# One fused kernel (long convolution and gated dense block) with its instructions in another order

## The chip, the cores and the metric

The kernel runs on one core of a Trainium2 chip. The core has five engines that run side by side, each through its own queue in the order in which the program issues to it: TensorE (PE, matmuls and transposes, which write to PSUM), VectorE (DVE), ScalarE (ACT), GpSimd (POOL) and SyncE (SP, which here only issues DMAs). They wait for each other through semaphores. The metric is the time of one execution on the device, in microseconds (us).

## The reference, cut to what matters

```python
def _A_ref(q, k, v, shift_k, ssm_k, ssm_D):          # S = 2048, D = 640
    k_pad = jnp.pad(k, ((0, 0), (ks - 1, 0), (0, 0)))            # ks = 4
    for t in range(ks):
        k_shift = k_shift + k_pad[:, t:t + S, :] * shift_k[:, ks - 1 - t][None, None, :]
    kv = k_shift * v
    # y = causal convolution of kv with ssm_k along S, by FFTs of length 2 S
    y = y + kv * ssm_D[None, None, :]
    return q * y
def _B_ref(x, w1, b1, w2):                           # F = 1728
    h = jnp.einsum("bsd,df->bsf", x, w1) + b1
    sp = jnp.log1p(jnp.exp(-jnp.abs(h))) + jnp.where(h > 0, h, jnp.zeros_like(h))
    return jnp.einsum("bsf,fd->bsd", h * jnp.tanh(sp), w2)
h = x + _A_ref(_layernorm(x, axis=-1), A_k, A_v, A_shift_k, A_ssm_k, A_ssm_D)    # x = A_q
h2 = h + _B_ref(_layernorm(h, axis=-1), B_w1, B_b1, B_w2)
return h2
```

## The kernel before

The program first builds a list of named steps (`OP(name, engines, dependencies, psum, ...)`), each of which issues one or a few instructions. Then `_ordered` reads the text `ORDER` and emits the steps one after the other in exactly that order, which fixes the order of every engine's queue and of the DMA queue. A token is a step's name. `@n` says which of four PSUM slots of 1024 float32 columns a PE step writes to; `:a`, `:d` or `:p` puts a step on ACT, DVE or POOL where the first of its listed engines isn't meant. A step that reuses a slot waits until the step that copies the old contents out of it is done. The names, in the order of the computation (dc, m and b count five groups of 128 channels, t counts 16 tiles of 128 positions):

- `d_n`, `d_k`, `d_v`, `d_g`, `d_x`, `d_t2m`, `d_a12`, `d_w1`, `d_w2`: loads (L319) of ssm_k, k, v, the table of the second Fourier stage in eight parts, x, two more tables and the weights.
- `dadd`, `k1pe`, `k1ev`: ssm_D is added to the first tap, ssm_k is transposed on PE (L370) and copied out.
- `s1kpe`, `s1kev`, `s2kpe`, `s2kev`: the two Fourier stages of the filter on PE (L390, L391 and L416), each with a copy out of PSUM by ACT (L256) or DVE (L258). Every step of s2k needs all twenty copies of s1k.
- `ktpe`, `ktev`, `ktsh`, `kspe`, `kv`: k is transposed (L335) and copied, one shifted copy is made on POOL, the short convolution runs as matmuls (L351, L352) with weights that `coef` and `wsh0` to `wsh3` (L311) build, and `kv` multiplies with v (L356).
- `s1vpe`, `s1vev`, `s2v0`, `s2v1`, `s2v2`: the same two stages for kv, the second in three chunks of channels (groups 0 and 1, group 2, groups 3 and 4).
- `sw`: two DMAs per group (L444) swap even and odd partitions of the filter's transform; they wait for all of s2k. `pr`: the product of both transforms, four steps per group on DVE (L455).
- `i1pe`, `i1ev`, `i2pe` (`i2a`, `i2b`), `y`: the two inverse stages (L473, L525) and their copies.
- `ln1`, `ln1p`, `lnx`: statistics and layer norm of x; `wb`, `h`, `bn`, `pow`, `hc`: product with it, residual, and second layer norm of a tile; `tr` (by DMA, L557) or `trpe` and `trev` (tiles 0 and 1): its transpose.
- `m1pe`, `hb`, `m2pe`, `res`, `d_out`: first dense layer (L582, L589) in five units of 256, 256, 512, 512 and 512 positions, Mish on ACT (L604), second dense layer (L647, L655), residual (L669, L672) and store.

Of the kernel before, what the change touches and what calls it, by code (L numbers as in the profile page):

```python
# [25 lines left out]
ORDER = """
d_dr wz idn d_n0 cz wm@0 small lane d_n1 d_cst d_sk d_n2 warm d_n3 d_n4 kz dsel d_g3 dcol dadd0 d_k0 k1pe0@1 d_k3 dadd1 k1pe1@2 d_k1 k1ev0 d_k2 k1ev0b
s1kpe0_0@3 k1ev1 s1kpe0_3@0 s1kev0_0 dadd2:p d_v3 s1kpe0_1@1 s1kev0_3 s1kev0_1:d s1kpe0_2@2 dadd3:p d_g6 s1kpe1_0@3 s1kev0_2 k1pe2@0 dadd4:p d_g7
s1kev1_0 cfpe@1 k1pe3@2 coef k1ev2:a s1kpe1_3@3 k1ev3 wsh0 k1pe4@1 d_v0 s1kev1_3 s1kpe2_0@0 k1ev4 s1kpe2_1@2 d_v2 s1kev2_0 wsh2 s1kpe3_0@3 s1kpe4_3@1
s1kev2_1 s1kev3_0:d s1kpe4_0@0 d_v1 s1kev4_3 s1kpe2_2@2 s1kev4_0:d wsh1 s1kpe3_1@3 s1kev2_2 ktpe2_0@1 d_g1 ktpe2_3 s1kev3_1:d ktpe4_0@0 ktpe4_1  # L30
ktpe1_0@2 ktpe4_3 ktpe1_1 wsh3 d_g0 ktpe4_2 ktpe1_2 ktev4 ktpe1_3 ktpe2_2 ktpe2_1 ktpe3_0@3 ktev2:a ktpe3_1 d_g4 ktev1 ktsh4 ktpe3_3 ktpe3_2
s1kpe3_2@0 ktev3 ktsh1 s1kpe4_1@2 d_g2 s1kev3_2 ktpe0_0@1 ktpe0_1 ktsh3 ktpe0_2 s1kev4_1 s1kpe1_2@3 d_g5 ktsh2 s1kpe1_1@0 s1kev1_2:d ktpe0_3 s1kev1_1
kspe3_1@2 ktev0 s1kpe4_2@3 s1kpe2_3@0 s1kev4_2 kv3_1 ktsh0 s1kpe3_3@1 s1kev2_3:d kspe4_0@3 s1kev3_3 kspe3_0@2 kv4_0 s2kpe_126@0 s2kpe_102@1
s2kev_126:d s2kpe_18@3 s2kev_102 kv3_0 kspe2_0@0 s2kev_18 s2kpe_0@1 kv2_0 s2kpe_48@2 s2kev_0 kspe0_0@3 s2kev_48 s2kpe_24@0 kv0_0 kspe1_0@1 s2kev_24
s2kpe_96@2 kv1_0 s2kpe_54@3 s2kev_96 kspe2_1@0 s2kev_54:d d_x0 s2kpe_36@1 d_x1 s2kpe_6@2 s2kev_36 kv2_1 kspe1_1@3 s2kev_6 s2kpe_66@1 kv1_1 s2kpe_84@0
s2kev_66 kspe4_1@2 s2kev_84 s2kpe_120@3 kv4_1 s2kpe_42@1 s2kev_120 kspe0_1@0 ln1_2 s2kev_42 s2kpe_72@2 s1vpe2_3@3 s2kev_72 kv0_1 ln1p2 s2kpe_60@1
s1vev2_3 s2kpe_30@2 s2kev_60:d d_x3 s1vpe0_1@0 s2kev_30 s1vpe2_0@3 s1vev0_1:d s1vpe1_2@1 s1vev2_0 s1vpe0_0@2 s1vev1_2:d s1vpe1_3@0 s1vev0_0
s2kpe_114@3 s1vev1_3 ln1_0 s1vpe3_0@2 s2kpe_12@1 s2kev_114 s1vev3_0:d s2kpe_108@0 s2kev_12 s2kpe_78@3 s2kev_108:d s2kpe_90@2 s2kev_78 s1vpe2_2@1
s2kev_90:d s1vpe0_2@0 s1vev2_2 lnx2:p s1vpe4_1@3 ln1p0 s1vev0_2 sw0_0 s1vpe1_1@2 s1vev4_1:d s1vpe0_3@1 sw1_1 s1vev1_1 s1vpe1_0@0 ln1_1 d_a12
s1vpe3_2@3 sw0_1 s1vev0_3 s1vpe2_1@2 sw3_1 s1vev1_0:d lnx0:p s1vev3_2 sw1_0 s1vpe4_2@1 ln1_3 sw4_1 ln1p1 s1vpe3_3@0 s1vev2_1 s2v0pe_80@3 sw3_0  # L40
s1vev4_2 s1vev3_3:d sw2_1 s2v0pe_64@2 ln1p3 sw2_0 s2v0ev_64 s2v0pe_96@1 s2v0ev_80:d s2v0pe_48@0 lnx3:p s2v0ev_96 s2v0pe_16@2 pr0_64 lnx1:p s1vpe4_3@3
s2v0ev_48 s1vpe3_1@1 s1vev4_3:d s2v0ev_16 s1vpe4_0@0 s1vev3_1 pr1_64 s2v0pe_0@2 s2v0pe_112@3 s1vev4_0 s2v0pe_32@1 s2v0ev_0:d s2v0ev_112 s2v2pe_0@0
pr0_0 s2v2pe_32@2 s2v2ev_0 pr0_96 s2v0ev_32 s2v2pe_96@3 s2v2ev_32 pr1_32 s2v1pe_96@0 s2v2ev_96 s2v1pe_32@1 pr1_0 s2v1ev_96 s2v2pe_16@2 pr1_96
s2v1pe_64@3 s2v1ev_32 s2v1pe_0@0 s2v2ev_16 pr0_32 i1pe1_3@1 s2v1ev_64 pr2_96 s2v1ev_0 s2v2pe_64@2 s2v2pe_112@3 i1ev1_3:d s2v2ev_64 s2v2pe_48@0 pr2_0
s2v2pe_80@1 s2v2ev_48 i1pe0_1@2 d_w11 s2v2ev_112 pr3_0 sw4_0 i1pe0_3@0 d_w10 i1ev0_1 pr2_32 i1pe1_2@3 d_x2 s2v2ev_80 d_w13 i1pe1_0@2 d_t2m pr2_64
i1ev0_3 d_w12 i1pe0_2@1 d_w14 pr3_96 i1ev1_0 i1pe1_1@0 i1ev1_2 pr3_32 i1pe0_0@2 i1ev1_1 pr3_64 i1pe2_0@3 i1ev0_0 i1pe2_3@0 pr4_64 i1ev0_2 i1pe3_0@2
pr4_96 i1ev2_3 i1pe3_2@1 i1ev3_0 pr4_32 i1pe2_2@0 i1ev3_2 pr4_0 i1pe3_1@2 i1ev2_0 i1pe2_1@1 ln1_8 i1ev2_2 i1pe3_3@3 ln1_5 i1ev3_1 ln1p8 i1pe4_3@0
i1ev2_1 ln1_7 i1pe4_2@2 ln1p5 i1ev4_3 ln1_6 i1pe4_1@1 lnx5:p i1ev3_3 i1pe4_0@0 i1ev4_2:d ln1p7 i1ev4_1 i2a0@3 d_w2b ln1_11 b1pe@2 i1ev4_0 i2a1@1 d_w2c
ln1p6 d_w2a ln1_12 c_b1 i2b0 i2b1 i2pe10@0 y0 i2a2@2 y1 wb0 i2b2 i2pe7@3 h0 y10 wb1 i2pe15@1 y2 h1 i2pe9@0 y7 bn1 i2a3@2 y9 i2pe14@3 y15 bn0 i2b3 pow1
i2pe6@0 y3 i2pe5@1 y6 wb2 i2pe11@2 pow0 hc1 y5 wb3 trpe1@0 y11 i2pe8@1 hc0 h3 trev1:a trpe0@2 bn3 trev0:a i2pe4@0 y14 m1pe0_4@2 h2 pow3 y8 bn2 lnx7  # L50
ln1p12 m1pe0_6@3 m1pe0_3@1 hc3 hb0_6 ln1_4 hb0_4 tr3 pow2 m1pe0_0@3 hb0_3 lnx6:p hc2 wb7 lnx8 tr2 m1pe0_1@2 ln1p11 ln1_10 hb0_0 m1pe0_2@1 hb0_1 h7
ln1p10 ln1_15 m1pe0_5@3 hb0_2 ln1p4 bn7 lnx12 m1pe1_3@2 hb0_5 wb5 ln1p15 m1pe1_0@1 ln1_13 hb1_3 lnx11 m1pe1_5@3 wb6 ln1p13 h6 y4 m1pe1_4@2 bn6 hb1_5
lnx15:p lnx4 m1pe1_2@0 h5 pow7 ln1_9 hb1_4 pow6 m1pe1_1@3 hb1_0 wb4 w2z hb1_2 m1pe1_6@2 hc7 bn5 tr7 lnx10:p hb1_1 i2pe12@1 hb1_6 h4 i2pe13@0 wb8 y12
m2pe1@3 h8 bn4 lnx13 y13 wb11 pow4 hc6 h11 pow5 hc4 ln1_14 ln1p9 tr4 m2pe3@2 bn11 ln1p14 tr6 lnx9 hc5 pow11 bn8 lnx14 tr5 wb12 pow8 wb14 m2pe0@1 res3
wb10 d_out3 wb15 hc11 hc8 tr11 h10 h12 m1pe2_5@0 wb9 bn10 bn12 pow10 m1pe2_4@2 hb2_5 h9 pow12 hc10 wb13 tr10 h13 m1pe2_0@0 bn9 hb2_4 tr8 h14 pow9 bn13
m1pe2_3@2 hb2_0 hc9 pow13 hc12 tr9 bn14 m2pe2@0 hb2_3 tr12 hc13 pow14 res1 hc14 d_out1 h15 tr13 bn15 pow15 m1pe2_6@2 res2 res0 d_out2 hc15 d_out0
m1pe2_1@3 hb2_6 tr14 tr15 m1pe3_6@0 m1pe3_4@1 hb3_6 m1pe2_2@2 hb3_4 hb2_1 m1pe3_1@0 hb2_2 m1pe3_2@1 hb3_1 m1pe3_3@3 m1pe3_5@2 hb3_3 m1pe3_0@0 hb3_5
hb3_2 m2pe4@3 hb3_0 m2pe6@2 m2pe5@1 res6 res4 d_out4 d_out6 m2pe7@0 m1pe4_6@2 res5 res7 d_out5 d_out7 m1pe4_5@3 hb4_6 m1pe4_3@1 m1pe4_1@0 hb4_3 hb4_5
m1pe4_4@2 hb4_1 m1pe4_2@1 hb4_4 m1pe4_0@3 hb4_2 m2pe9@0 hb4_0 m2pe11@2 m2pe15a@1 res9 res11 d_out11 d_out9 m2pe8@3 res15a d_out15a m2pe10@0 m2pe12@2
res8 res10 d_out8 d_out10 m2pe14@1 m2pe13@3 res12 res14 d_out12 d_out14 m2pe15b@0 res13 d_out13 res15b d_out15b  # L60
""".split()
# [656 lines left out]
```

## Time and profile before

| what | value |
|---|---|
| median of 3 runs | 227.34 us (227.21 to 227.75) |
| the profiled execution | 227.22 us |
| its span | 225.2 us |
| granted TensorE clock | 1.00 in every stretch |
| busy: PE, DVE, ACT, POOL | 214.5, 137.9, 131.8, 51.4 us |
| loaded from and written to HBM | 20.42 and 2.62 MB |

The span is counted from the first to the last instruction of the profile; about 2 us lie around it. Times in the profile are from the start of the span. A row of a timeline has the start, the duration, the engine, the line and the operation, with output and inputs and their shapes, a count for rows that were merged, and in brackets how long the engine stood idle before it and for whom. In the chain of work that ended last, a row is the start, the duration and what ran; the chain goes back from the last instruction to what released it. Ends of matmuls are modelled.

### The profile page before, as it was taken

The numbers are of one execution on the slowest core, as the hardware profiler recorded it, in microseconds if no ns is written. First come the engines' busy times: TensorE is split into PE (matmuls) and PEld (weight loads), VectorE is DVE, ScalarE is ACT, GpSimd is POOL, SyncE is SP. The second block draws the span as 40 slices with busy tenths as digits, with TensorE's granted clock in tenths as the row PEclk, the third lists the DMA queues.
The fourth block names the chain that finished last, engine by engine and source line by source line (L and its number), as shares of the span: only waits on it lengthen the run. The fifth ranks groups of instructions, "written<-read, shape, count | busy, mean of one in ns | idle before, by whom it ended". The sixth has DMA issues, their size and how long they took to land.

```text
span 225.2 us, 6200 instructions
## 1 busy us (share of the span) xinstructions
PE 214.5 (95%) x2684; PEld 157.5 (70%) x2690; DVE 137.9 (61%) x250; ACT 131.8 (59%) x180; POOL 51.4 (23%) x102
## 2 busy tenths in 40 slices
...
DMA packets 19563, 30.98 MB, mean 138 GB/s; under 512 B 10704, under 2 KB 14928, under 8 KB 18768
## 3 DMA queue, kind: packets, MB, share of 16 engines
...
q10 hardware_dynamic: 336, 0.12, 0.3%
...
HBM read 20.42 MB, written 2.62 MB: 102 GB/s over the span
## 4 chain that ended last, share of the span: by engine, by line
PE 69%; DVE 9%; ACT 8%; issue 6%; DMA 5%; POOL 1%; SPq 1%; DVEq 0%; ACTq 0%
PE ps L647 26%; PE ps L582 25%; ACT uv L256 5%; PE ps L473 4%; PE ps L390 3%; ACT ks L256 3%; DVE ra L356 3%; DVE ks L455 3%; DMA ks<-ks 3%; PE ps L335 2%; DMA ks<-in_A_ssm_k_dram 2%; PE ps L370 2%; DVE uv L258 2%; PE ps L589 1%; PE ps L655 1%
## 5 line engine op out<-in xcount | busy, mean ns | idle before, releaser
L604 ACT ACTIVATE ks<-ps,b1s 128x512 bf16<-128x512 f32 (+1 forms) x69 | 35.9, 605 | 43.2 <-PE ps L589 22.9
L647 PE MATMUL ps<-ks 128*128 128x320 bf16 (+2 forms) x420 | 58.6, 299 | 0.0
L582 PE MATMUL ps<-G 128*128 128x512 bf16 (+1 forms) x319 | 57.2, 336 | 0.4
L672 DVE TENSOR_TENSOR rb<-ps,rb 128x640 bf16<-128x640 f32 x15 | 11.8, 819 | 68.3 <-PE ps L655 65.9
L647 PEld LDWEIGHTS <-ks 128*128 128x128 bf16 x420 | 40.6, 98 | 17.4 <-issue 1.3
L582 PEld LDWEIGHTS <-G 128*128 128x128 bf16 x325 | 31.4, 98 | 24.5 <-issue 1.4
L256 ACT CAST uv<-ps 128x1024 bf16<-128x1024 f32 x49 | 45.5, 1089 | 0.5 <-ACT uv L256 0.4
L256 ACT CAST ks<-ps 128x960 bf16<-128x960 f32 (+2 forms) x47 | 39.0, 910 | 8.6 <-PE ps L391 6.1
L455 DVE TENSOR_TENSOR ks<-ks,uv 128x2048 bf16<-128x2048 bf16 x20 | 23.1, 1218 | 1.2 <-DMA ks<-ks 1.2
L416 PEld LDWEIGHTS <-G 128*128 128x128 bf16 x512 | 20.5, 96 | 4.5 <-issue 3.8
L473 PE MATMUL ps<-a_t,ks 128*128 128x128 bf16 x320 | 18.2, 219 | 0.8 <-DVE ks L455 0.8
L473 PEld LDWEIGHTS <-ks 128*128 128x128 bf16 x320 | 18.0, 113 | 0.9 <-DVE ks L455 0.9
L542 POOL TENSOR_TENSOR r<-ve,mhalf 128x1 f32<-128x1 f32 x16 | 10.5, 661 | 22.7 <-DVE ve L540 22.7
L416 PE MATMUL ps<-uv,G 128*128 128x64 bf16 (+1 forms) x384 | 12.4, 187 | 2.5 <-DVE uv L258 1.9
L538 DVE BATCH_NORM_STATS2 st<-rb 128x6 f32<-128x320 bf16 x32 | 14.0, 479 | 0.2
L509 POOL TENSOR_SCALAR ve<-mv 128x1 f32<-128x1 f32 x16 | 4.2, 260 | 43.2 <-DVE mv L505 42.1
L504 DVE BATCH_NORM_STATS2 st<-rb 128x6 f32<-128x320 bf16 x32 | 13.8, 473 | 0.0
L258 DVE CAST uv<-ps 128x1024 bf16<-128x1024 f32 x11 | 13.0, 1202 | 0.2 <-ACT uv L256 0.2
L258 DVE CAST ks<-ps 128x1024 bf16<-128x1024 f32 (+2 forms) x11 | 12.1, 1126 | 1.6 <-PE ps L391 1.6
L356 DVE TENSOR_TENSOR ra<-ps,rb 128x1024 bf16<-128x1024 f32 x10 | 12.0, 1219 | 1.2 <-PE ps L352 0.9
L416 PE MATMUL ps<-ks,G 128*128 128x160 bf16 x128 | 11.2, 230 | 0.6 <-DVE ra L356 0.2
L390 PE MATMUL ps<-cst,ra 128*64 128x128 bf16 x160 | 11.0, 219 | 0.5 <-ACT uv L256 0.4
...
## 6 DMA issues: line engine op xcount, KB each, us to landing
ks<-ks SPq DMA_DIRECT2D x10, 512.0 KB, 6.0
G<-tab_g SPq DMA_DIRECT2D x8, 512.0 KB, 11.3
ks<-in_A_ssm_k_dram SPq DMA_DIRECT2D x5, 512.0 KB, 6.1
...
```

Source lines behind the costliest of these rows:

```text
L256: nc.scalar.copy(o, i)
L258: nc.vector.tensor_copy(o, i)
L356: nc.vector.tensor_tensor(kv_w[:, m, :, 8 * h:8 * h + 8, :], p_.f32().rearrange("p (l t d) -> p d t l", l=4, t=8), raw_v[:, 8 * h:8 * h + ...
L390: nc.tensor.matmul(ps[0:64, dgl, :], lhs, mc, start=True, stop=True)
L416: nc.tensor.matmul(p_.f32()[:, o:o + n], g_v[:, f, :], src[:, :, f, :], start=True, stop=True)
L455: nc.vector.tensor_tensor(o, o, v, ALU.mult)
L473: nc.tensor.matmul(pz[:, dgl, :], KS[:, k, b, :, l], a12[:, k, :], start=k == 0, stop=k == 1)
L504: nc.vector.bn_stats(st1[:, t, hh, :], xt(t)[:, hh * 320:(hh + 1) * 320])
L538: nc.vector.bn_stats(st2[:, t, hh, :], xt(t)[:, hh * 320:(hh + 1) * 320])
L582: nc.tensor.matmul(ph[:, o:o + w], w1[:, dc, fc * P:fc * P + P], lt[:, dc, 0:w], start=dc == 0, stop=dc == NDC - 1)
L604: nc.scalar.activation(hb[:, fc, 0:n], p_.f32()[:, i * 512:i * 512 + n], ACT.Mish, bias=b1s[:, fc:fc + 1], scale=1.0)
L647: nc.tensor.matmul(p_.f32()[:, o:o + n], lhs, w2[:, k, cols:cols + n], start=fc == 0, stop=single and fc == 13)
```

## The change

`ORDER` is replaced. The steps are the same, each issues the same instructions, and each engine gets as many steps as before (214 on PE, 166 on DVE, 145 on ACT, 56 on POOL, 76 DMAs of SP). Different are the order in which they are issued, the PSUM slot of most PE steps, and the engine of some: the copies that DVE makes are others than before (16 go from DVE to ACT and 14 from ACT to DVE, i1 and before), `wsh2` moves from POOL to DVE, `dadd1` from DVE to POOL, `dadd2` and `dadd3` from POOL to DVE, `lnx10` from POOL to ACT and `lnx4`, `lnx11` and `lnx14` from ACT to POOL. The loads go out in the order n0 n1 n3 n2 n4 g2 k1 k0 k2 k3 v0 g4 g0 v1 v3 v2 g1 a12 g5 g6 g3 g7 where it was n0 to n4 g3 k0 k3 k1 k2 v3 g6 g7 v0 v2 v1 g1 g0 g4 g2 g5. The last part, from `m2pe14` on, has the same order. Cut to the part up to m1 in the new text (the old text: up to the first steps of s2k):

```diff
 ORDER = """
-d_dr wz idn d_n0 cz wm@0 small lane d_n1 d_cst d_sk d_n2 warm d_n3 d_n4 kz dsel d_g3 dcol dadd0 d_k0 k1pe0@1 d_k3 dadd1 k1pe1@2 d_k1 k1ev0 d_k2 k1ev0b
-s1kpe0_0@3 k1ev1 s1kpe0_3@0 s1kev0_0 dadd2:p d_v3 s1kpe0_1@1 s1kev0_3 s1kev0_1:d s1kpe0_2@2 dadd3:p d_g6 s1kpe1_0@3 s1kev0_2 k1pe2@0 dadd4:p d_g7
-s1kev1_0 cfpe@1 k1pe3@2 coef k1ev2:a s1kpe1_3@3 k1ev3 wsh0 k1pe4@1 d_v0 s1kev1_3 s1kpe2_0@0 k1ev4 s1kpe2_1@2 d_v2 s1kev2_0 wsh2 s1kpe3_0@3 s1kpe4_3@1
-s1kev2_1 s1kev3_0:d s1kpe4_0@0 d_v1 s1kev4_3 s1kpe2_2@2 s1kev4_0:d wsh1 s1kpe3_1@3 s1kev2_2 ktpe2_0@1 d_g1 ktpe2_3 s1kev3_1:d ktpe4_0@0 ktpe4_1
-ktpe1_0@2 ktpe4_3 ktpe1_1 wsh3 d_g0 ktpe4_2 ktpe1_2 ktev4 ktpe1_3 ktpe2_2 ktpe2_1 ktpe3_0@3 ktev2:a ktpe3_1 d_g4 ktev1 ktsh4 ktpe3_3 ktpe3_2
-s1kpe3_2@0 ktev3 ktsh1 s1kpe4_1@2 d_g2 s1kev3_2 ktpe0_0@1 ktpe0_1 ktsh3 ktpe0_2 s1kev4_1 s1kpe1_2@3 d_g5 ktsh2 s1kpe1_1@0 s1kev1_2:d ktpe0_3 s1kev1_1
-kspe3_1@2 ktev0 s1kpe4_2@3 s1kpe2_3@0 s1kev4_2 kv3_1 ktsh0 s1kpe3_3@1 s1kev2_3:d kspe4_0@3 s1kev3_3 kspe3_0@2 kv4_0 s2kpe_126@0 s2kpe_102@1
-s2kev_126:d s2kpe_18@3 s2kev_102 kv3_0 kspe2_0@0 s2kev_18 s2kpe_0@1 kv2_0 s2kpe_48@2 s2kev_0 kspe0_0@3 s2kev_48 s2kpe_24@0 kv0_0 kspe1_0@1 s2kev_24
...
+d_dr wz idn d_n0 cz wm@0 small lane d_n1 d_cst d_sk d_n3 warm d_n2 d_n4 d_g2 dsel dcol dadd0 d_k1 k1pe0@1 d_k0 dadd1:p k1pe1@2 d_k2 k1ev0b d_k3 k1ev0
+s1kpe0_3@3 k1ev1 s1kpe0_2@0 s1kev0_3 d_v0 s1kpe0_0@1 dadd3 s1kev0_2 s1kpe0_1@2 dadd2 d_g4 k1pe3@3 s1kev0_1 k1pe2@0 dadd4:p d_g0 s1kev0_0 k1ev3 kz
+cfpe@2 k1ev2:a k1pe4@1 coef s1kpe3_0@3 d_v1 k1ev4 wsh1 s1kpe1_1@2 s1kev3_0 s1kpe3_2@0 s1kev1_1:d s1kpe1_0@1 s1kev3_2 d_v3 s1kpe4_0@3 wsh0 s1kev1_0
+s1kpe2_2@2 s1kev4_0:d s1kpe2_0@0 d_v2 s1kpe1_2@1 s1kev2_0 s1kev2_2:d ktpe0_0@3 ktpe0_1 wsh3 s1kev1_2 s1kpe4_2@0 d_g1 wsh2:d ktpe4_0@2 s1kev4_2
+ktpe1_0@1 ktpe4_2 ktpe1_1 ktpe0_2 d_a12 ktpe4_1 ktpe4_3 ktpe2_0@0 ktev4 ktpe0_3 ktpe2_2 ktpe2_1 d_g5 ktpe2_3 ktev0 ktpe1_2 ktev2:a ktpe3_0@2 ktpe3_3
+ktpe3_2 ktpe1_3 d_g6 ktsh0 s1kpe2_1@3 ktev1 ktsh4 ktpe3_1 s1kev2_1 s1kpe2_3@0 d_g3 ktev3 s1kpe4_1@1 ktsh1 s1kev2_3 kspe4_0@3 ktsh2 s1kev4_1 ktsh3 d_g7
+kspe1_0@2 kv4_0 s1kpe1_3@0 s1kpe3_1@1 kv1_0 s1kev1_3 s1kpe4_3@3 s1kev3_1 s1kpe3_3@0 s1kev4_3:d kspe1_1@2 s1kev3_3 kspe0_0@1 kv1_1 s2kpe_36@3
+s2kpe_24@0 kv0_0 s2kev_36 kspe3_1@2 s2kev_24 s2kpe_12@3 kv3_1 kspe2_0@1 s2kev_12 s2kpe_78@0 kv2_0 kspe0_1@2 s2kev_78 kspe2_1@3 kv0_1 s2kpe_102@1
+s2kpe_30@0 kv2_1 s2kev_102 kspe3_0@2 s2kev_30 s2kpe_60@1 kv3_0 s1vpe0_0@3 s2kev_60 s1vpe1_3@0 s1vpe0_3@2 d_x0 s1vev0_0 s1vev1_3:d kspe4_1@1 s1vev0_3
+s2kpe_126@3 s1vpe0_2@0 kv4_1 s2kev_126 s1vpe0_1@2 s1vev0_2 s1vpe1_0@3 s1vev0_1:d d_x2 s1vpe1_2@1 s1vev1_0 d_x3 s1vpe1_1@0 d_x1 s1vev1_2:d s1vpe4_1@2
+s1vev1_1 d_t2m s2kpe_90@3 s1vev4_1 ln1_1 s2kpe_0@1 s2kpe_66@0 s2kev_0 s2kpe_6@2 s2kev_90:d ln1p1 s2kev_6 s2v0pe_96@1 s2kev_66:d s2v0pe_16@3 s2v0ev_96
+s2kpe_72@2 s2v0ev_16:d s2kpe_48@0 s2kev_72 s2kpe_96@1 s2kev_48 s2kev_96:d s2kpe_84@3 s2kpe_120@2 s2kev_84 s2kpe_42@0 s2kev_120:d s2kpe_54@1 s2kev_42
+s2kpe_108@3 s2kev_54:d s2kpe_114@2 s2kev_108 s1vpe3_1@0 s2kev_114 s1vpe3_0@1 s1vev3_1:d s2kpe_18@3 s1vev3_0 s2v0pe_48@2 s2kev_18:d s2v0pe_80@0
+s2v0ev_48 s2v0pe_64@1 ln1_0 s1vpe3_2@3 sw1_1 s2v0ev_80 s2v0pe_0@2 sw1_0 s1vev3_2:d s2v0ev_64 ln1p0 s1vpe3_3@0 sw3_1 sw0_0 s2v0ev_0 ln1_2 s1vpe2_2@1
+sw3_0 s1vpe4_2@3 s1vev2_2 s1vpe4_3@2 sw0_1 s1vev3_3:d ln1p2 sw2_1 s1vev4_3 s1vpe4_0@1 sw4_0 ln1_3 s2v0pe_32@0 s1vev4_0 sw2_0 s1vpe2_0@2 s2v0ev_32:d
+sw4_1 ln1p3 s1vev4_2 s1vpe2_3@1 s1vev2_3 pr1_0 s2v2pe_16@3 lnx3:p s2v0pe_112@0 s1vev2_0 s1vpe2_1@1 pr1_32 s2v2ev_16 lnx1:p s2v2pe_0@2 s2v0ev_112:d
+s1vev2_1 lnx0:p s2v2pe_96@3 s2v2ev_0 pr1_64 lnx2:p s2v2pe_64@0 s2v2pe_48@1 s2v2ev_64 s2v1pe_32@2 pr1_96 s2v2ev_96 pr0_96 i1pe1_2@0 s2v1ev_32 i1pe1_0@3
+pr0_32 i1ev1_2 i1pe1_1@2 i1ev1_0 pr0_64 s2v2ev_48 pr3_0 s2v2pe_32@0 i1ev1_1 s2v1pe_0@3 pr0_0 s2v2ev_32 s2v1pe_64@1 pr2_32 s2v1ev_0 s2v2pe_80@2
+s2v1pe_96@0 s2v1ev_64 pr3_32 s2v2pe_112@3 s2v1ev_96 i1pe0_0@1 d_w12 pr2_0 d_w13 s2v2ev_80 i1pe0_1@0 d_w10 pr2_96 s2v2ev_112 d_w11 i1pe1_3@2 d_w14
+pr2_64 i1ev0_1 i1pe0_2@3 i1ev0_0 pr3_64 i1pe2_2@0 i1ev1_3 i1pe2_0@1 pr3_96 i1ev2_2 i1pe2_3@2 pr4_0 i1ev2_0 i1pe3_1@0 i1ev0_2 pr4_64 i1pe3_3@1 i1ev2_3
+pr4_96 i1pe3_2@3 i1ev3_3 i1pe0_3@2 ln1_4 i1ev3_1 i1pe2_1@1 pr4_32 ln1p4 i1ev3_2 i1pe3_0@0 i1ev2_1 ln1_7 lnx4:p i1pe4_3@3 i1ev3_0 ln1_6 ln1p7 i1pe4_0@1
+i1ev0_3 i1pe4_2@0 ln1_5 ln1p6 i1ev4_0 i1pe4_1@2 i1ev4_3:d i1ev4_2 i2a0@1 w2z d_w2b ln1_9 i1ev4_1 b1pe@3 i2a3@0 d_w2a ln1p5 d_w2c c_b1 ln1_10 i2b0
+i2a1@2 y0 i2b1 i2pe4@3 y1 wb0 i2b3 i2pe12@1 h0 y4 wb1 i2pe13@2 y3 bn0 i2pe15@3 y12 i2pe5@0 y15 h1 i2pe14@1 pow0 y13 bn1 i2a2@3 lnx6:p y14 i2b2 i2pe8@2
+y2 wb3 i2pe6@1 pow1 hc0 y8 i2pe7@3 wb2 y5 trpe0@2 hc1 h3 trev0:a trpe1@0 bn3 trev1:a i2pe11@2 y7 m1pe0_4@0 h2 pow3 y6 bn2 lnx7 lnx5:p m1pe0_3@3 hc3
+hb0_4 pow2 m1pe0_5@1 ln1_14 tr3 y11 ln1p10 hb0_3 m1pe0_0@0 hc2 wb5 tr2 ln1p9 lnx10 ln1_13 m1pe0_6@2 m1pe0_1@3 hb0_5 wb7 ln1p13 hb0_0 ln1_8 m1pe0_2@1
+h7 ln1p8 m1pe1_2@0 ln1_11 hb0_2 hb0_1 m1pe1_3@1 wb4 ln1p11 h4 hb1_2 m1pe1_0@3 bn7 hb0_6 lnx11:p lnx8 m1pe1_1@0 bn4 ln1p14 hb1_3 hb1_0 m1pe1_5@2 h5
+pow4 lnx9 ln1_15 m1pe1_4@1 pow7 hb1_1 wb11 lnx14:p m1pe1_6@3 hb1_5 hc4 wb6 ln1p15 tr4 hb1_4 ln1_12 i2pe9@0 hb1_6 i2pe10@2 bn5 ln1p12 m2pe1@1 y10 y9 h6
...
```

33 lines of the change are left out of this document (7 added, 26 removed).

## Prediction

> **What bounds the kernel now.** I read the page first, then busy time by stretches, then the chain of work that ended last, then the timelines of ScalarE (ACT), VectorE (DVE) and the DMA queue.
>
> ```profile
> span 225.2 us, 6200 instructions
> PE 214.5 (95%) x2684; PEld 157.5 (70%) x2690; DVE 137.9 (61%) x250; ACT 131.8 (59%) x180; POOL 51.4 (23%) x102
> 8.63:37.22 28.59, 27.97 (x598) 26.58 (x593) 23.91 (x25) 22.40 (x23) 11.97 (x12) 1.00 0.87 353
> 37.22:91.38 54.16, 50.02 (x1152) 46.69 (x1149) 51.78 (x65) 53.66 (x59) 11.22 (x25) 1.00 0.63 229
> 101.17:222.24 121.07, 120.74 (x815) 75.17 (x820) 49.93 (x127) 44.90 (x82) 22.58 (x43) 1.00 0.14 40
> ```
>
> The 95% of PE on the second line is an average over two different kernels. In a row of stretches stand the length, then busy PE, PEld, DVE, ACT, POOL. From 101.17 to 222.24, where the two dense layers run, PE is busy 120.74 of 121.07 us: nothing but its own work ends last there, and no order can gain there. From 37.22 to 91.38 it is ACT, busy 53.66 of 54.16, that copies results out of PSUM; DVE has 51.78. From 8.63, ACT's first copy, to 37.22 ACT is idle 28.59 - 22.40 = 6.19 us. That idle time is what an order can win or lose. The chain shows the handover:
>
> ```profile
> 86.87 5.77 ACT uv L256 x6
> ...
> 92.68 0.29 PE ps L525 x2
> 92.99 0.70 ACT ks L256
> ...
> 100.43 0.70 ACT G L256
> 101.17 14.35 PE ps L582 x130
> ```
>
> So the time is: when ACT gets its last copy of i1 away (the last of the x6 row, which ends at 92.64; it starts 1.25 earlier, and I count by that start, 91.38), plus a fixed chain from there over y0, the layer norm of tiles 0 and 1 and two transposes to the first m1 matmul at 101.17, plus 121.1 us of PE, plus the last residual. After PE's end the new order has the same steps as the old, so nothing changes there.
>
> **Paces.** All durations of the walk below come from these rows.
>
> ```profile
> 8.63 3.76 ACT L256 CAST ks<-ps 128x1024 bf16<-128x1024 f32 x4 [4.62 <-PE ps L391]
> 21.60 1.86 ACT L256 COPY uv<-ps 128x2048 bf16<-128x2048 bf16 x1 [2.46 <-PE ps L335]
> 30.82 5.74 ACT L256 CAST ks<-ps 128x960 bf16<-128x960 f32 x6 [1.27 <-PE ps L416]
> 37.22 6.18 ACT L256 CAST ks<-ps 128x960 bf16<-128x960 f32 x7 [0.66 <-PE ps L416]
> 75.12 17.51 ACT L256 CAST uv<-ps 128x1024 bf16<-128x1024 f32 x19 [0.39 <-ACT uv L256]
> 92.99 6.66 ACT L256 CAST ks<-ps 128x640 bf16<-128x640 f32 x11 [0.28 <-PE ps L525]
> 31.21 2.36 DVE L356 TENSOR_TENSOR ra<-ps,rb 128x1024 bf16<-128x1024 f32 x2
> 55.05 0.87 DVE L504 BATCH_NORM_STATS2 st<-rb 128x6 f32<-128x320 bf16 x2
> 56.09 2.30 DVE L258 CAST uv<-ps 128x1024 bf16<-128x1024 f32 x2
> 18.44 4.14 PE ps L335 x64
> 31.53 0.06 PE ps L351
> ...
> 32.22 0.06 PE ps L351
> 32.32 0.83 PE ps L416 x12
> 74.14 7.49 PE ps L473 x135
> ```
>
> A copy of 1024 columns (s1, s2v, i1) holds ACT for (3.76 - 1.04) / 3 = 0.905 us, one of 960 (s2k) for (6.18 - 1.02) / 6 = 0.86; a y copy (6.66 - 0.7) / 10 = 0.59. A DVE step on 1024 columns takes 2.36 - 1.21 = 1.15. An ln1 takes 56.09 - 55.05 = 1.04. A ktpe (four transposes) holds PE for 4.14 / 16 = 0.26, a kspe for about 0.8 (eight pairs, 0.1 apart), an s2kpe (six matmuls) for 0.83 / 2 = 0.42, an i1pe (sixteen of 7.49 / 135) for 0.89. The 2.46, 1.27 and 0.66 in brackets are most of ACT's 6.19 us of waits. I carried the new order through these paces step by step: PE starts a step when the copy that last held its PSUM slot (the number behind @) is done, and a copy may start when its last matmul has ended in the trace (92.68 + 0.29, then 92.99 in the chain).
>
> **Loads.** The new order fetches k and g in another sequence, from the same queue.
>
> ```profile
> G<-tab_g SPq DMA_DIRECT2D x8, 512.0 KB, 11.3
> 24.00:28.00 4.00, 3.92 (x98) 3.51 (x98) 2.93 (x4) 2.95 (x4) 1.59 (x3) 1.00 1.01 413
> 17.92 5.85 SPq L319 DMA_DIRECT2D G<-tab_g  x5
> ```
>
> The engines of the DMA are full (share 1.01, 413 GB/s), so landing follows the cumulated bytes: the last g lands near 23.4 + 11.3 = 35 in both orders. In the new one I find no user that comes before its load: s2kpe_60, which needs g3, runs at 37.1 and g3 lands near 34; kv4_0 needs v0 and v1, near 25, and runs at 26. I cost the loads at nothing, covered by the copies of s1k; without that cover a g that is late by 1 us would cost 1 us. The small moves cost nothing either: dadd1 on POOL and dadd2, dadd3 on DVE touch one column, which each k1pe transposes last; lnx4, lnx11 and lnx14 on POOL and lnx10 on ACT lie in the stretch from 101.17 on, where POOL is busy for 22.58 of 121 us. On the DMA queue all d_x and d_t2m now stand in front of the swaps; the last of them waits for s1vpe1_1 (42.6), long before the swaps, and the d_w behind the swaps wait for the last s2v steps (74), 26 us before m1.
>
> **ACT, 8.6 to 37.** The new order moves copies between the engines: 16 of s1k on ACT where there were 14, and only 5 of s2k by 37 where there were 6. Work done by then: 2 x 0.905 - 0.86 = 0.95 us more. The waits, from the walk: 2.1 for ktev2, since eleven ktpe (11 x 0.26) stand between s1kev1_2, which frees slot 1 at 19.2, and ktpe2_3; 0.6 for s1kev1_3; 1.0 for s2kev_36, the first of s2k, which needs all of s1k (the last, s1kev3_3, ends at 30.2); 1.15 for s2kev_102, whose step stands behind kspe0_1 and kspe2_1 (from 33.9, when s2kpe_78 is through, 2 x 0.8 + 0.42 and PE's tail of 0.2 make 36.1, and ACT is free at 35.0); 0.35 in small ones. That is 5.2 against 6.19. ACT comes to s2kev_30 at 37.1, as before to s2kev_36 at 37.22.
>
> **ACT, 37 to the last i1.** Left in the new order are 11 copies of s2k, one of them short (9.0 us), and 14 + 17 + 19 of s1v, s2v and i1 (50 x 0.905 = 45.25): 54.25. In the old: 11 x 0.86 + 49 x 0.905 = 53.8, so 0.45 more is left. Waits here: the old order has 54.16 + 0.9 - 53.8 = 1.3 against this pace; my walk of the new one finds 0.2, because each i1pe result is ready 0.5 us ahead of ACT's turn, and only s1vev4_0 and s1vev2_3 are ready within 0.1 us of it. These are the two ends; I take 0.6, between them, since a walk misses small delays. The last i1 copy then starts at 37.1 + 54.25 - 0.9 + 0.6 = 91.0 against 91.38: -0.4 (bounds -0.8 and +0.3).
>
> **DVE beside it.** The product pr1_0 waits for a swap of partitions that DMAs make (L444).
>
> ```profile
> 51.67 1.17 SPq L444 DMA_DIRECT2D ks<-ks  x2
> ks<-ks SPq DMA_DIRECT2D x1, 512.0 KB, 5.7
> 53.63 8.47 SPq L444 DMA_DIRECT2D ks<-ks  x7
> 53.63 5.80 DMA ks<-ks
> 59.55 1.23 DVE L455 TENSOR_TENSOR ks<-ks,uv 128x2048 bf16<-128x2048 bf16 x1 [1.16 <-DMA ks<-ks]
> 67.69 2.36 DVE ks L455 x2
> ```
>
> The first two swaps went out at 51.67 and near 52.3; the second (the row with 5.7) landed at 58.0, the third, out at 53.63, at 59.4, and DVE stood 1.16 for it. In the new order all s2k is copied only at 53.8 (s2kev_18 on DVE: thirteen steps from s1vev1_3 at 38.8, 14.6 us at 1.12 each, and 0.4 of waits), 2.1 later, but the first two swaps are both of group 1, the first that pr needs, and lie in front of d_w and behind d_t2m, which is long issued (43). They land at 53.8 + 6.3 = 60.1. DVE has six steps in between (three ln1, three copies: 3 x 1.04 + 3 x 1.15 = 6.6) and is at pr1_0 at 60.3, its last step overlapping. Then 20 pr at 2.36 - 1.22 = 1.14, one copy and one ln1: 85.3. The step that needs the last of them, i1pe4_3, has its turn on PE at 85.9. So the wait of 1.16 goes, and what is late next is ACT.
>
> **Handover.** From y0 to the first m1: old 101.17 - 92.99 = 8.18. New: DVE has wb0 h0 wb1 bn0 h1 bn1 wb3 hc0 wb2 hc1, the same ten steps as before in another order, and hc1 is last in place of hc0; ACT has 11 copies (6.45) in front of trev0 as before. I get 8.05: -0.1.
>
> **The dense layers.** The same PE work, with i2pe9 and i2pe10 left over in place of i2pe12 and i2pe13. PE is full there, so a change can only add a wait. The tightest place is hb0_5, which stands behind lnx10 on ACT, which needs pow2 and ln1p10 on POOL: ready about 0.1 us before m1pe0_2 wants its slot. Cost 0 to 0.3; I take 0.1. The transposes tr4 to tr7 come no later: from wb0 to the last hc of this unit DVE has one wb more, one h and one bn fewer than before.
>
> **wsh2** moves from POOL to DVE.
>
> ```profile
> 13.04 8.14 POOL L311 TENSOR_TENSOR rw<-cst,coef 128x1120 bf16<-128x1120 bf16 x4 [1.69 <-DVE coef L303]
> L532 DVE TENSOR_TENSOR ks<-ks,ra 128x640 bf16<-128x640 bf16 x16 | 7.5, 477 | 0.7 <-ACT ks L256 0.7
> L542 POOL TENSOR_TENSOR r<-ve,mhalf 128x1 f32<-128x1 f32 x16 | 10.5, 661 | 22.7 <-DVE ve L540 22.7
> L510 POOL TENSOR_TENSOR r<-ve,mhalf 128x1 f32<-128x1 f32 x16 | 9.0, 564 | 1.3
> ```
>
> No row shows it on DVE: between 0.48 (640 columns) and 2.04 (POOL, 8.14 / 4). I take 1.2, nearest to the DVE step on 1024 columns; it starts at 18.5 and ktev4, next on DVE, can't start before 21.0, when its transposes are done. At 2.04 it would still be hidden. On POOL wsh1, wsh0 and wsh3 run from coef's end at 13.5 to 13.6 + 3 x 2.04 = 19.7, beside it. What DVE and POOL cost each other, L542 and L510 show: the same pow takes 661 ns among the two-input DVE steps wb and h, and 564 elsewhere, 0.1 us more. The Trainium skill, "SBUF — State Buffer", section "Who interferes with whom", is stricter: a DVE instruction with two SBUF inputs and a GpSimd instruction that reads SBUF exclude each other for their whole length. By it wsh2 would start at 19.7; the 0.1 us in the trace is far less than a whole wb of 0.48.
>
> **Sum.** -0.4 - 0.1 + 0.1 = -0.4. The profiled execution took 227.22 (span 225.2 and 2.0 around it), 0.12 under the median of 227.34, so the sum gives 226.8 for such an execution and 226.9 for the median. About 0.3% (0.68 us) is what a measurement of this kernel can tell from no change; the forecast lies inside that, near its lower edge.
>
> **Rivals.** (1) ACT's walk holds to its lower bound: -0.8, handover -0.1, no wait in m1: -0.9, and up to -1.3 if the early waits are shorter by the 0.35 of small ones; 226.3. For it: the rules of the walk give each wait of the old trace that I tried. Against: two copies with margins of 0.1. Chance 0.33. (2) wsh2 is blocked: it runs from 19.7 and, at the upper bound of 2.04 us and a late start of its own, ends at 21.9; ktev4, due at 21.0, and all that DVE does up to kv and s2k come 0.9 later. -0.4 + 0.9 = +0.5, 227.8. It decides once wsh2 ends after 21.0. For it: the pair that the 661 ns show. Against: 0.1 us there. Chance 0.08. (3) Slower: the two swaps of group 1 land late. In the old order the fourth swap landed 8.9 us after the first had been issued (seven go out in the 8.47 us from 53.63, so the fourth near 54.9, and lands like the one above 5.7 later, against 51.67). If the eight that follow share the DMA engines so that the second of group 1 lands like that, pr1_0 starts at 62.7, 2.4 late; i1pe4_3 has 0.6 of slack, and everything from the last i1 on comes 1.8 later: -0.4 + 1.8 = +1.4, 228.7. For it: the first four swaps landed in bunches. Against: both of group 1 go out first. It decides from a landing after 60.9. Chance 0.20. The forecast itself, -0.68 to +0.68 with its middle at -0.4, has 0.39.
>
> **How the numbers follow.** Faster by over 0.3% is (1) and the edge that the forecast shares with it, 0.38. Within 0.3% is the rest of the forecast and most of (2), less what falls to waits that I can't name, 0.36. Slower is (3) and these, 0.26. The range goes from (1)'s far end, -1.3, to a little over (3): 226.0 to 228.8; the forecast's own runs from 226.5 to 227.6.
>
> **What would show it.** Right: ACT's wait at ktev2 about 2 us, at the first s2k about 1, almost none from 37 to the last i1 copy, which starts near 91.0; pr1_0 near 60.3 without a wait on the swaps; first m1 8.1 us after y0, near 100.6; PE full from there. Wrong: ACT idle over 1.5 us after 37, DVE waiting on the swaps, or PE waiting on hb or a transpose after m1 has begun.

## The result, and the profile after

| kernel | median, us | ratio to before, 95% interval | runs |
|---|---|---|---|
| before | 227.32 (227.08 to 228.17) | | 20 |
| after | 227.14 (226.74 to 227.60) | 0.9987 [0.9981, 0.9993] | 20 |

The new order is 0.13% faster, 0.3 us by the ratio and 0.2 us by the medians. That is within the 0.3% that count as no change, and inside the forecast's own range of 226.5 to 227.6; the forecast was 226.9. The profiled execution took 227.16 us.

The head of the page after. Each engine's row has busy time, share of the span and number of instructions:

```profile
span 225.4 us, 6189 instructions
PE 215.8 (96%) x2690; PEld 158.0 (70%) x2690; DVE 139.5 (62%) x250; ACT 131.3 (58%) x180; POOL 60.4 (27%) x102
```

The surprise is POOL: 60.4 us where it had 51.4, with the same 102 instructions. DVE has 139.5 for 137.9. Busy time by stretches, from ACT's first copy to its first s2k past 37, on to the last i1 copy, to the first m1 matmul, and to PE's end (length, then busy PE, PEld, DVE, ACT, POOL):

```profile
8.94:37.56 28.62, 28.16 (x611) 26.87 (x606) 25.10 (x26) 23.33 (x24) 9.50 (x14) 1.00 0.87 353
37.56:91.60 54.04, 50.44 (x1140) 46.95 (x1137) 52.91 (x64) 53.86 (x61) 20.25 (x25) 1.00 0.65 237
91.60:101.17 9.57, 8.92 (x68) 5.05 (x67) 8.80 (x25) 9.29 (x17) 5.54 (x10) 1.00 0.23 82
101.17:222.40 121.23, 121.18 (x821) 75.12 (x820) 49.03 (x127) 43.34 (x80) 22.19 (x42) 1.00 0.16 40
```

The same four stretches had 28.59, 54.16, 9.79 and 121.07 us before. The last one ends here where the last residual starts (222.40) and there at PE's end (222.24); to the residual it was 121.10 before. ACT's first copy itself came at 8.94 for 8.63. That start follows the second load of ssm_k: in every trace it comes 1.9 us after that load has landed (here 7.05, then 8.94). It moves from execution to execution: seven experiments below with the same first steps show 8.55 to 9.51. So I count all times from ACT's first copy (the last i1 copy starts at 91.62 in its own row below, 0.02 behind the cut above; "PE's end" is the start of the last residual, 0.02 behind it):

| from ACT's first copy to | before | after | difference | predicted |
|---|---|---|---|---|
| first s2k past 37 | 28.59 | 28.62 | +0.03 | -0.1 |
| last i1 copy, start | 82.75 | 82.68 | -0.07 | -0.4 |
| y0 | 84.36 | 84.19 | -0.17 | -0.4 |
| first m1 matmul | 92.54 | 92.23 | -0.31 | -0.5 |
| PE's end | 213.64 | 213.46 | -0.18 | -0.4 |

The last line, -0.18, agrees with the -0.2 to -0.3 of the timed runs. ACT's timeline after, for the waits (in brackets the idle time before a row and whom it waited for):

```profile
8.94 3.76 ACT L256 CAST ks<-ps 128x1024 bf16<-128x1024 f32 x4 [4.93 <-PE ps L391]
...
22.44 1.87 ACT L256 COPY uv<-ps 128x2048 bf16<-128x2048 bf16 x1 [2.06 <-PE ps L335]
...
27.96 2.84 ACT L256 CAST ks<-ps 128x1024 bf16<-128x1024 f32 x3 [0.79 <-PE ps L391]
31.84 3.79 ACT L256 CAST ks<-ps 128x960 bf16<-128x960 f32 x4 [1.04 <-DVE ra L356]
36.66 2.68 ACT L256 CAST ks<-ps 128x960 bf16<-128x960 f32 x3 [1.03 <-PE ps L416]
...
80.76 12.01 ACT L256 CAST uv<-ps 128x1024 bf16<-128x1024 f32 x13 [0.18 <-PE ps L473]
...
93.13 6.66 ACT L256 CAST ks<-ps 128x640 bf16<-128x640 f32 x11 [0.28 <-PE ps L525]
```

The four early waits are the predicted ones: 2.06 for 2.1 (ktev2), 0.79 for 0.6 (s1kev1_3), 1.04 for 1.0 (s2kev_36) and 1.03 for 1.15 (s2kev_102). After 37 one wait of 0.18 is left, at 80.76; where it comes from is the story below. The chain of work that ended last:

```profile
88.00 4.78 ACT uv L256 x5
92.82 0.29 PE ps L525 x2
93.13 6.66 ACT ks L256 x11
99.79 0.63 ACT G L256
100.46 0.70 PE ps L525 x4
101.17 6.13 PE ps L582 x55
107.31 8.35 PE ps L582 x75
...
222.40 0.42 DVE rb L669
```

From y0 to m1 it is 101.17 - 93.13 = 8.04 (8.05 was predicted). The m1 row, one row of x130 before, is cut in two at 107.31: there PE waited, at m1pe0_2.

What the prediction didn't name is on POOL and DVE. First POOL's timeline, then the views of the two lines, L455 (the products pr) and L518 (the layer norms lnx), with shortest, median and longest duration in ns:

```profile
61.28 11.49 POOL L518 TENSOR_SCALAR ra<-rb,r,nmr 128x640 bf16<-128x640 bf16 x4
```

```profile
L455 DVE TENSOR_TENSOR ks<-ks,uv x20: 1172/1210/1739, 61.0 to 86.2; 128x2048 bf16<-128x2048 bf16 x20
```

```profile
L518 POOL TENSOR_SCALAR ra<-rb,r,nmr x10: 864/876/3948, 61.3 to 119.5; 128x640 bf16<-128x640 bf16 x10
```

Four lnx took 11.49 us where one takes 0.87 alone, and three of the 20 pr took 1.55 to 1.74 where the median is 1.21. (One of the four lnx, which began beside a copy out of PSUM on DVE, took 0.86; the others took 2.77 to 3.95.) In the new order lnx3, lnx1, lnx0 and lnx2 stand among the pr; in the old one all four were through before the first pr. PE's timeline shows who paid:

```profile
79.58 11.82 PE L473 MATMUL ps<-a_t,ks 128*128 128x128 bf16 x208 [0.65 <-DVE ks L455]
```

PE waited for a product of group 2 (i1pe2_2), ACT then for PE.

### The profile page after: what moved, and what is told of

Same layout as the page of the kernel before. It is cut to its first block, busy times and chain, and to the rows that moved or that the text cites. A ratio compares the mean times of both kernels' runs of the same rounds, so it can differ in the third digit from the quotient of the medians.

```text
span 225.4 us, 6189 instructions
## 1 busy us (share of the span) xinstructions
PE 215.8 (96%) x2690; PEld 158.0 (70%) x2690; DVE 139.5 (62%) x250; ACT 131.3 (58%) x180; POOL 60.4 (27%) x102
## 4 chain that ended last, share of the span: by engine, by line
PE 68%; ACT 16%; DVE 10%; DMA 2%; issue 2%; SPq 0%; ACTq 0%; DVEq 0%
PE ps L647 26%; PE ps L582 25%; ACT uv L256 10%; DVE ks L455 7%; ACT ks L256 5%; PE ps L416 3%; PE ps L390 3%; DMA ks<-in_A_ssm_k_dram 2%; PE ps L335 2%; PE ps L351 2%; DVE ks L258 2%; PE ps L352 1%; PE ps L589 1%; PE ps L655 1%; PE ps L370 1%
## 5 line engine op out<-in xcount | busy, mean ns | idle before, releaser
L582 PE MATMUL ps<-G 128*128 128x512 bf16 (+1 forms) x325 | 57.8, 337 | 0.0
L256 ACT CAST uv<-ps 128x1024 bf16<-128x1024 f32 x50 | 46.5, 1141 | 0.2 <-PE ps L473 0.2
L256 ACT CAST ks<-ps 128x1024 bf16<-128x1024 f32 (+3 forms) x48 | 39.1, 902 | 8.7 <-PE ps L391 5.9
L455 DVE TENSOR_TENSOR ks<-ks,uv 128x2048 bf16<-128x2048 bf16 x20 | 24.3, 1278 | 0.0
L509 POOL TENSOR_SCALAR ve<-mv 128x1 f32<-128x1 f32 x16 | 5.3, 329 | 43.9 <-DVE mv L505 43.0
L518 POOL TENSOR_SCALAR ra<-rb,r,nmr 128x640 bf16<-128x640 bf16 x10 | 16.9, 1697 | 0.3
L416 PE MATMUL ps<-uv,G 128*128 128x64 bf16 (+1 forms) x384 | 12.9, 186 | 1.6 <-ACT uv L256 1.3
L258 DVE CAST uv<-ps 128x1024 bf16<-128x1024 f32 x10 | 12.0, 1206 | 0.6 <-ACT ks L256 0.6
L258 DVE CAST ks<-ps 128x960 bf16<-128x960 f32 (+1 forms) x10 | 11.5, 1174 | 0.1
```

Of the source, the lines that this page charges most:

```text
L256: nc.scalar.copy(o, i)
L258: nc.vector.tensor_copy(o, i)
L416: nc.tensor.matmul(p_.f32()[:, o:o + n], g_v[:, f, :], src[:, :, f, :], start=True, stop=True)
L455: nc.vector.tensor_tensor(o, o, v, ALU.mult)
L518: nc.gpsimd.tensor_scalar(lnx_s[t % 9], xt(t), r1[:, t:t + 1], nmr1[:, t:t + 1], ALU.mult, ALU.add)
L582: nc.tensor.matmul(ph[:, o:o + w], w1[:, dc, fc * P:fc * P + P], lt[:, dc, 0:w], start=dc == 0, stop=dc == NDC - 1)
```

## Experiments

Each is the new order with some tokens moved. Ratios are to the kernel before, run in the same session. "To the end" is the time in the trace from ACT's first copy to the start of the last residual, which leaves out the chance of the start. The median of before was 227.3 to 227.6 in these sessions, so the ratios compare better than the medians. The new order itself was timed in the first session only; e2 to e5 share a second one, e1 and e6 to e8 a third. And a trace is one execution: against before, the last column lies 0.3 to 0.6 us above what the ratios give (1.1 for e1, 0.1 for after). So the traces show where a run gains or loses; a size from them is no surer than that.

| run | change to the new order | median, us | ratio to before, 95% interval | y0 | to the end |
|---|---|---|---|---|---|
| before | | 227.32 | | 84.36 | 213.64 |
| after | | 227.14 | 0.9987 [0.9981, 0.9993] | 84.19 | 213.46 |
| e2_lnx_late | lnx0 to lnx3 behind the products | 226.78 | 0.9969 [0.9958, 0.9980] | 83.95 | 213.24 |
| e3_i1_dve | one more i1 copy on DVE | 227.43 | 1.0005 [0.9993, 1.0017] | 84.17 | 214.30 |
| e4_both | e2 and e3 | 226.96 | 0.9974 [0.9962, 0.9986] | 83.33 | 213.56 |
| e5_all | e4, lnx10 later | 227.00 | 0.9984 [0.9971, 0.9997] | 83.33 | 213.56 |
| e1_old_loads | loads in the old sequence | 230.34 | 1.0111 [1.0088, 1.0133] | 87.98 | 217.28 |
| e6_wsh2_alone | wsh2 behind ktev4 | 228.19 | 1.0023 [1.0010, 1.0036] | 85.40 | 214.68 |
| e7_wsh2_pool | wsh2 on POOL | 227.21 | 0.9980 [0.9960, 1.0000] | 84.52 | 213.81 |
| e8_late_lnx10 | e2, lnx10 later | 226.76 | 0.9954 [0.9938, 0.9970] | 83.91 | 213.02 |

**Are POOL's layer norms what slows the products?** lnx0 to lnx3 go behind the last pr; lnx4 moves on to keep POOL's queue free.

```diff
-pr1_0 ... lnx3:p ... pr1_32 ... lnx1:p ... lnx0:p ... pr1_64 lnx2:p
-ln1p4 i1ev3_2 ... ln1_7 lnx4:p
+pr1_0 ... pr1_32 ... pr1_64
+ln1p4 lnx0:p lnx1:p lnx3:p lnx2:p i1ev3_2 ... ln1_7
-ln1p10 hb0_3
+ln1p10 lnx4:p hb0_3
```

> The new order, but on POOL lnx0 to lnx3 stand behind ln1p4, so that they run after the products pr and not beside them (lnx4 goes behind ln1p10 to make room). Theory: beside the two-input products POOL's lnx took 2.8 to 3.9 us in place of 0.87, and four products 0.3 to 0.5 us longer, 1.4 us of DVE in all; but ACT and PE have as much left to do, so only ACT's wait of 0.18 us at i1ev2_2 goes: products back to 1.14 us each, PE's wait of 0.8 us at i1pe2_2 gone, time 0.2 us below the new order, near 227.0. Rival A: the lost time on DVE was on the path; then 0.8 to 1.4 us less, near 226.0. Rival B: the two engines don't disturb each other and the long rows on POOL are an artefact; then no row of DVE changes.

The views of the two lines, the timeline of POOL and that of PE in this run:

```profile
L455 DVE TENSOR_TENSOR ks<-ks,uv x20: 1173/1212/1226, 60.8 to 84.8; 128x2048 bf16<-128x2048 bf16 x20
```

```profile
L518 POOL TENSOR_SCALAR ra<-rb,r,nmr x10: 863/870/1112, 87.0 to 120.4; 128x640 bf16<-128x640 bf16 x10
```

```profile
87.04 3.45 POOL L518 TENSOR_SCALAR ra<-rb,r,nmr 128x640 bf16<-128x640 bf16 x4
```

```profile
74.89 15.72 PE L473 MATMUL ps<-a_t,ks 128*128 128x128 bf16 x272 [0.28 <-ACT uv L256]
```

No product takes over 1.23 us, the four lnx take 3.45 us for 11.49, and PE runs all the i1 steps from 74.89 on in one row: its wait for a product is gone. The first theory holds in cause. In size the traces give 213.46 - 213.24 = 0.22 us (0.2 was expected); the ratios give 0.4, over two sessions. By the starts of the last product in the two views DVE was through 1.1 us earlier (86.2 - 8.94 against 84.8 - 8.67), and only 0.22 of that reached the end. PE's wait took 0.65 of the 1.1; the rest met slack on PE. What became of the 0.65 is in ACT's copies. ACT's timeline of this run, in two narrow stretches:

```profile
52.65 1.09 ACT L256 CAST uv<-ps 128x1024 bf16<-128x1024 f32 x1
```

```profile
90.73 1.53 ACT L256 CAST uv<-ps 128x1024 bf16<-128x1024 f32 x1
```

These are the first and the last of 43 copies in a row without a wait. From 52.65 to 90.73 a copy begins every 38.08 / 42 = 0.907 us, but the ends, from 53.74 to 92.26, are 38.52 / 42 = 0.917 apart, so that the last copy takes 1.53. Its consumer on PE waits for the end. In the new order the wait at 80.76 had let this lag drain. Three of its copies, just ahead of the wait, just behind it, and the last:

```profile
79.22 1.35 ACT L256 CAST uv<-ps 128x1024 bf16<-128x1024 f32 x1
```

```profile
80.76 1.01 ACT L256 CAST uv<-ps 128x1024 bf16<-128x1024 f32 x1 [0.18 <-PE ps L473]
```

```profile
91.62 1.16 ACT L256 CAST uv<-ps 128x1024 bf16<-128x1024 f32 x1
```

So the last copy starts 82.68 - (90.73 - 8.67) = 0.62 us earlier in e2, takes 1.53 - 1.16 = 0.37 longer, and y0 comes 0.24 earlier. A wait that goes, here the 0.65 us on PE, is thus worth less than it looks.

**Does ACT's last part get shorter with a copy moved to DVE?** The copy i1ev4_2 goes from ACT to DVE, and four layer-norm steps move back to make room for it:

```diff
-i1pe4_2@0 ln1_5 ln1p6 i1ev4_0 i1pe4_1@2 i1ev4_3:d i1ev4_2 i2a0@1 w2z d_w2b ln1_9
+i1pe4_2@0 i1ev4_3:d ln1p6 i1ev4_0 i1ev4_2:d ln1_5 i1pe4_1@2 i2a0@1 w2z d_w2b
+hc3 ln1_9
+wb5 ... ln1_14
+ln1p13 ln1p9
```

> The new order, but i1ev4_2 is copied by DVE in place of ACT, which takes 0.905 us off ACT ahead of y0 (ln1_9 and ln1_14 move to a later place on DVE to make room). Theory: in the last stretch of i1 PE is as full as ACT (i1pe2_2 starts 0.8 us late for pr2, then 13 steps of 0.89 to 91.2), so the last copy can start at 91.4 at the earliest, not 91.6: 0.2 us less, near 226.9. Rival: ACT alone bounds this stretch; then 0.9 us less, near 226.2.

> Both edits together. Theory: PE gets to i1pe2_2 0.8 us earlier and ACT has one copy less, so the last i1 copy starts near 90.6 in place of 91.6, and y0 and the first m1 come about 0.9 us earlier: near 226.2, more than the sum of the two alone (0.4). Rival A (ACT alone bounds): the same as the copy edit alone plus 0.2. Rival B (POOL chain or DVE chain to the first m1 takes over, since lnx0 to lnx3 now end near 91.5 and w2z and ln1p5 behind them): y0 comes earlier, but hc0 or hc1 doesn't, and less than 0.4 us is left.

> Both edits, and on ACT lnx10 stands behind hb0_0 in place of ahead of hb0_5. Theory: in the new order lnx10 waits 0.47 us for ln1p10, hb0_5 ends at 107.24 and m1pe0_2 takes 1.25 in place of 1.08 us for its PSUM slot; without that PE has no wait from the first m1 on: 0.15 us below the kernel with both edits, near 226.0, and PE busy all the time from the first m1 to its end. Rival: another copy comes late in its place and nothing changes.

All three missed their times. The profiled execution of e3 is the longest of its twelve (228.55 for a median of 227.43), and it was late before the edit could matter: DVE waited for a load of x. DVE's timeline of e3 in one row, and ACT's in two:

```profile
45.13 0.89 DVE L504 BATCH_NORM_STATS2 st<-rb 128x6 f32<-128x320 bf16 x2 [0.17 <-DMA rb<-in_A_q_dram]
```

```profile
81.64 10.18 ACT L256 CAST uv<-ps 128x1024 bf16<-128x1024 f32 x11 [0.37 <-PE ps L473]
92.31 1.01 ACT L256 CAST uv<-ps 128x1024 bf16<-128x1024 f32 x1 [0.50 <-PE ps L473]
```

ACT's wait behind the late product ends 81.64 - 9.51 = 72.13 us after its first copy, 0.31 later than in the new order (80.76 - 8.94 = 71.82). From there to y0 e3 needs 12.04 us for 12.37. So y0, the same in both, hides a gain of 0.3 from the moved copy, about what the theory gave, and no more than that because ACT now waited for PE ahead of the last i1 copy. The loss comes behind y0: from y0 to the end e3 takes 130.13 us for 129.27.

In e4, with the products at full speed, y0 came 84.19 - 83.33 = 0.86 earlier, as planned, and all of it was given back by PE's end (213.56 for 213.46; by the ratios e4 lies between the new order and e2). Rival B had the size, but not the place: the first m1 matmul still came 0.6 earlier. The chain that ended last in e4 and PE's timeline beside it:

```profile
120.21 0.27 POOL nmr L511
120.50 0.93 ACT ra L516
121.45 0.72 DVE ks L532
...
129.21 0.40 DVE rb L534
129.61 0.75 DVE rb L672
130.40 3.40 PE ps L582 x15
```

```profile
130.40 3.40 PE L582 MATMUL ps<-G 128*128 128x512 bf16 x15 [0.22 <-DVE rb L672]
```

In this stretch the chain isn't on PE but on the layer norms of later tiles, POOL to ACT to DVE, down to a residual on DVE, and PE waits for that. DVE is full there too. The stretches of the new order from 103 to 133 (DVE is the third number after the length):

```profile
103.00:113.00 10.00, 9.99 (x93) 8.79 (x91) 9.66 (x31) 8.92 (x23) 8.20 (x20) 1.00 0.15 34
...
123.00:133.00 10.00, 10.00 (x64) 5.67 (x63) 9.72 (x28) 1.27 (x2) 2.00 (x3) 1.00 0.22 50
```

So the 1.2 us of the copy and the steps that were moved back came out again; which of the two it was isn't shown, since no run moved one alone. Against e2, e4 lost 130.23 - 129.29 = 0.94 from y0 to the end: 0.2 ahead of m1, and then PE's steps start 0.12 later from m1pe1_4 on, 0.2 more from m2pe1 on and 0.38 more from m1pe2_1 on (the step that waits for the residual). e5, with lnx10 moved as well, has the same end as e4: what it gains at m1pe0_2 it waits for at m1pe1_4.

**Are the loads free in any sequence?** The new order with the old sequence of k, v and g:

```diff
-d_g2 d_k1 d_k0 d_k2 d_k3 d_v0 d_g4 d_g0 d_v1 d_v3 d_v2 d_g1 d_g5 d_g6 d_g3 d_g7
+d_g3 d_k0 d_k3 d_k1 d_k2 d_v3 d_g6 d_g7 d_v0 d_v2 d_v1 d_g1 d_g0 d_g4 d_g2 d_g5
```

> The new order, with the loads d_k, d_g and d_v in their old sequence (k0 k3 k1 k2, v3 first of v, g2 next to last); the steps keep their places. My theory: the loads are part of the order, not free. In the new order kv4_0 needs v0 and v1 near 26 and the first step of s2k, s2kpe_36, needs g2; with the old sequence v1 lands near 28.4 and g2 near 33.5, so kv4_0 and s2kpe_36 start later and everything behind them on DVE and PE too: 2.2 to 2.8 us slower than the new order, near 229.6. Rival: the landings are covered by the copies of s1k in any sequence: no difference, 227.1.

```profile
28.92 2.35 DVE L356 TENSOR_TENSOR ra<-ps,rb 128x1024 bf16<-128x1024 f32 x2 [2.99 <-ACT ks L256]
```

```profile
rb<-in_A_v_dram SPq DMA_DIRECT2D x2, 640.0 KB, 12.4
```

```profile
35.16 3.79 ACT L256 CAST ks<-ps 128x960 bf16<-128x960 f32 x4 [2.83 <-PE ps L416]
```

The first row is DVE's first kv step, which starts at 26.7 in the new order: 2.5 us later by ACT's first copy. The wait is put down to ACT, which had long been done; the cause that fits is v1, the last of the three v that go out from 12.5 to 16.4 us, which lands 12.4 after its issue, near 28.8. The last row is ACT's first s2k copy, 3.5 late. Its step, s2kpe_36, needs g2, but in this execution g2 wasn't the last to come. It goes out at 24.2 and lands 9.8 later, at 34.0; the step begins at 34.27, right behind two kspe steps, and these ran at half the clock (the number behind POOL's is the granted TensorE clock):

```profile
31.32:34.73 3.41, 3.41 (x36) 3.40 (x36) 2.46 (x3) 1.01 (x1) 0.00 (x0) 0.50 0.56 226
```

The two kspe take 34.27 - 31.32 = 2.95 us, for 31.18 - 29.60 = 1.58 in the new order, where the clock is 1.00 throughout. At the full clock they would have been through near 32.9, and g2 would have decided, about 0.3 us earlier than the step really began; that is an estimate from these rows. The other three executions had a mean clock of 1.00. The end is 213.46 to 217.28, 3.8 us later in this execution, the longest of four, and 2.8 by the ratios (2.2 to 2.8 was expected). The late v1 fits and the size is measured; what g2 alone costs isn't shown. So the sequence of loads is no side matter of this order: it is made for it.

**What made wsh2 take 2.30 us?** DVE's timeline of the new order, and the view of L311:

```profile
18.75 2.30 DVE L311 TENSOR_TENSOR rw<-cst,coef 128x1120 bf16<-128x1120 bf16 x1
21.20 2.36 DVE L258 COPY uv<-ps 128x2048 bf16<-128x2048 bf16 x2
```

```profile
L311 POOL TENSOR_TENSOR rw<-cst,coef x3: 2061/2066/2068, 13.8 to 17.8; 128x1120 bf16<-128x1120 bf16 x3
```

My bounds were 0.48 and 2.04. POOL's last wsh starts at 17.8 and ends at 19.87; wsh2 ends 1.18 later, at 21.05. In e2, where wsh2 began 0.2 earlier against POOL, it took 2.49 and again ended 1.18 after POOL's last. To take POOL's work away from it, wsh2 went behind ktev4 in one run, and back to POOL in another:

```diff
-wsh3 ... d_g1 wsh2:d ktpe4_0@2 ... ktev4 ktpe0_3
+wsh3 ... d_g1 ktpe4_0@2 ... ktev4 wsh2:d ktpe0_3
```

> The new order with wsh2, still on DVE, moved behind ktev4, where POOL has finished its own three wsh. If the 2.30 us that wsh2 took on DVE came from the wsh on POOL beside it, it takes 1.1 to 1.2 us here. If it is what this step takes on DVE, it takes 2.3 again. Time: wsh2 now lies between ktev4 and the next copies of DVE; half of the time that it takes comes out as delay, 0.5 us by the first theory (227.6), 1.2 by the second (228.3).

```profile
21.96 1.31 DVE L311 TENSOR_TENSOR rw<-cst,coef 128x1120 bf16<-128x1120 bf16 x1
```

```profile
25.14 2.90 ACT L256 CAST ks<-ps 128x1024 bf16<-128x1024 f32 x3 [1.20 <-PE ps L391]
```

Alone wsh2 takes 1.31 us, so the other 1.0 came from POOL. But uncovered it costs more than the half that was expected: in the trace ACT's next wait is 1.20 and the end 1.22 later, and by the ratios it is 0.8 us against the new order and 1.0 against e7, of the same session.

```diff
-wsh3 ... d_g1 wsh2:d ktpe4_0@2
+wsh3 ... d_g1 wsh2 ktpe4_0@2
```

> The new order with wsh2 back on POOL, in the same place of the text. The four wsh on POOL take 2.04 to 2.07 us each, as in the kernel before, and end near 21.9; kspe needs them from about 25. DVE is free of 2.30 us in front of ktev4, which waits for PE. If the move of wsh2 is hidden, as the prediction has it: no change, 227.1 +- 0.2. If the blocked DVE step cost time that the trace hides: 0.3 us or more faster.

No change that can be measured: 227.21 us, a ratio of 0.9980 with an interval that holds 0.9987. ktev4 starts 12.27 us after ACT's first copy, for 12.26: the move of wsh2 is hidden either way. The 0.35 by which e7's trace ends later begins at 44, where DVE waits for a load of x:

```profile
44.20 0.89 DVE L504 BATCH_NORM_STATS2 st<-rb 128x6 f32<-128x320 bf16 x2 [0.23 <-DMA rb<-in_A_q_dram]
```

ACT began early there (8.55), and the load didn't come earlier with it. At pr1_0 e7 is 0.16 late, and at the last product 0.32 (86.09 - 8.55 against 86.16 - 8.94). e3 has the same wait; after, e2, e4, e5 and e8 don't, and up to ACT's long row at 52.9 these five agree within 0.02 us. So the times from ACT's first copy, too, are no better than some 0.3 us where loads set the pace.

**The wait at m1pe0_2.** e2 with one more token moved:

```diff
-tr2 ln1p9 lnx10 ln1_13 m1pe0_6@2 m1pe0_1@3 hb0_5 wb7 ln1p13 hb0_0 ln1_8
+tr2 ln1p9 ln1_13 m1pe0_6@2 m1pe0_1@3 hb0_5 wb7 ln1p13 hb0_0 lnx10 ln1_8
```

> The new order with lnx0 to lnx3 behind the products, as in the experiment that did this alone, and with lnx10 on ACT moved from ahead of hb0_5 to behind hb0_0. hb0_5 then doesn't wait for the layer norm of tile 10, and the step m1pe0_2, which took 1.26 us for 1.09, takes 1.09. Theory: that is the last wait of the first unit and nothing later is late: 0.17 us less than lnx0 to lnx3 alone, near 226.6. Rival: as in the experiment with both moves, where the same 0.17 came back as a wait of m1pe1_6 for hb1_0: no gain, 226.8.

ACT's timeline after (first) and in e8 (second), and the chain of e8:

```profile
105.61 0.92 ACT L516 ACTIVATE ra<-rb,nmr,r 128x640 bf16<-128x640 bf16 x1 [0.47 <-POOL nmr L511]
```

```profile
104.14 2.35 ACT L604 ACTIVATE ks<-ps,b1s 128x256 bf16<-128x256 f32 x6
```

```profile
101.02 14.34 PE ps L582 x130
```

ACT's wait of 0.47 for POOL's statistics of tile 10 stood ahead of hb0_5. With lnx10 behind hb0_0 three hb (six instructions) run on without a gap, m1 is one row of x130 in the chain again, and the end comes 0.22 before e2 in the traces; by the ratios the two can't be told apart, since their intervals overlap. The rival had the wait of e5 in mind. It was m1pe1_4 that waited there, for hb1_3, and not m1pe1_6 for hb1_0; in e8 it doesn't come back. This is the fastest version: 0.9954 [0.9938, 0.9970] against 0.9987 [0.9981, 0.9993] of the new order; the two intervals don't meet.

## Why the prediction came out right

Its sum was -0.4 and the trace shows -0.18. The sum has an error of its own: 8.63 + 22.40 + 0.95 + 5.2 is 37.18 and not 37.1, and 37.18 + 54.25 - 0.9 + 0.6 = 91.13 lies 0.25 ahead of 91.38, not 0.4. With -0.1 and +0.1 behind it, its own terms give -0.25. Step by step:

- **ACT, 8.6 to 37.** The waits sum to 28.62 - 23.33 = 5.29 us for 5.2 predicted, against 6.19 before; the work is 23.33 - 22.40 = 0.93 more for 0.95. The step holds; it gave +0.03, since gain and extra work cancel.
- **ACT, 37 to the last i1.** In the bookkeeping of the prediction the waits are 54.04 + 0.9 - 54.25 = 0.69 for 0.6. The size is right and the reason was not: it was put down to small delays, and nearly all of it, 0.63 by the starts of the copies, is one break ahead of 80.76, where PE waited for a product. e2 takes that break away.
- **DVE beside it.** The swaps did what was said: they went out from 54.6 on, and pr1_0 started at 61.02 without waiting for them (60.3 predicted, 0.3 of the difference from the later start). Rival (3), slower by 1.4, didn't come. The failed step is the next one, 20 pr at 1.14 each: four lnx on POOL stand among them in the new order, the prediction didn't look at them, and the last pr came 1.1 us later than without them (e2). e2 prices this at 0.22 us at the end. -0.18 - 0.22 = -0.40 is the forecast's number, but partly by luck: in e2 ACT's waits after 37 come to 0.07 where 0.6 was allowed, the last copy takes 0.28 more than before (1.53 for 1.25), for which there was no term, and the sum had the error above.
- **Handover.** 8.04 us for 8.05. (The 6.45 for eleven copies beside it is 6.66 in the row shown there; the sum doesn't use it.)
- **The dense layers.** hb0_5 behind lnx10 was named as the tightest place, at 0.1 (0 to 0.3). PE's last stretch, to the residual in both, is 121.23 for 121.10, 0.13 more; e8 gets 0.22 back in its trace by moving lnx10.
- **Loads at nothing.** Right for k, v and g in the new sequence; a load of x made DVE wait 0.17 and 0.23 us in two of eight traces with this sequence (e3, e7). e1 shows the cover that it has: the old sequence under the same steps costs 2.8 us by the ratios, 3.8 in the profiled execution.
- **wsh2.** The term that was mis-sized: 2.30 us for 1.2, above the upper bound of 2.04. The conclusion held, since ktev4 came at 21.20 and no later (e7). Rival (2) had the mechanism right; it cost nothing because wsh2 needed only 1.18 us behind POOL's last wsh, not 2.04, and was through at 21.05. The reason given was wrong: the 0.1 us of the pow steps, on one column each, says nothing about long instructions. Here e6 and e2 agree with the Trainium skill, "SBUF — State Buffer", section "Who interferes with whom": a DVE instruction with two SBUF inputs and a GpSimd instruction that reads SBUF exclude each other for their whole length. By it wsh2 starts when POOL's last wsh ends, and 1.18 us of its own follow that end in both traces, after and e2 (alone it took 1.31). The same rule, applied to lnx and pr, names the contention that the prediction missed. Of the order in which the two get their turns, the Trainium skill says there that whoever issues first blocks the other; in the trace single lnx took up to 3.95 us, about three pr.
- **Rival (1)**, 226.3, needed ACT without waits after 37, and none in m1. e2 has the first, and its last i1 copy starts 82.75 - 82.06 = 0.69 us earlier than before, near the rival's 0.8. But that copy takes 1.53 us for 1.25, so y0 comes only 84.36 - 83.95 = 0.41 earlier: the lag of ACT's ends behind its starts is what the rival missed. e8 has both and ends 0.62 earlier in the trace; its ratio, 1.0 us with an interval from 0.7 to 1.4, doesn't rule out the rival's 0.9.
